# Attention and soft mixture of experts in one kernel: 2 MB transfers, half a weight tile loaded early, another order of the experts

## The chip, the cores and the metric

The kernel runs on one core of a Trainium2 chip. The metric is the device time of one execution in microseconds. Three runs of the kernel before took 131.04, 131.25 and 131.40 us; their median is 131.25 us.

## The reference

Eight batches, eight heads, 512 tokens and 32 state rows of 64 numbers each, all float32. Each token attends to the 32 state rows of its batch and head, and each state row attends to the 512 tokens. The results are laid side by side into 4608 rows of 512 numbers, (512 + 32) rows for each batch. A soft mixture of experts follows: 8 experts, 4 slots each, hidden size 1024.

```python
scores = scale * x @ state.T;  a = softmax(scores);   xread = a @ state
scores2 = scale * state @ x.T; a2 = softmax(scores2); sread = a2 @ x
z = concat([xread, sread])              # 4608 x 512
logits = z @ phi                        # 4608 x 32
slot_input = softmax(logits, axis=0).T @ z          # 32 x 512
for e in range(8):                      # 4 slots of each expert
    slot_out[e] = relu(slot_input[e] @ w1[e]) @ w2[e]
out = softmax(logits, axis=1) @ slot_out            # 4608 x 512
```

x is 8 MB, the weights w1 and w2 are 16 MB each, the output is 8.5 MB.

## The kernel before

**Stages.** Attention runs over batches 0 to 7 with its steps interleaved by hand: ORDER (lines 29 to 57) lists them as name.batch.half, and the loop at line 661 issues them in that order. `X.b.g` transposes a quarter of batch b on TensorE, `S.b` makes both kinds of scores, `R.b.h` multiplies the state rows' weights with x and is the last reader of batch b's x. The logits never leave the chip; the softmax over all rows is kept as a running maximum and sum. Every engine has its own queue and works through it in this order.

Then come the experts. `w1_part(hf, e)` multiplies one expert's slots with half of its w1 (a tile of 1 MB): 2 halves x 8 experts. Two results are kept in PSUM (`h_ps`), turned and rectified (`h_turn`, `h_relu`) into `h_m`, while VectorE, ScalarE and GpSimd make the softmax over slots (`c_max`, `c_exp`, `c_div`, `c_back`). `w2_part(k, hf, e)` then adds expert e's share to the slot outputs of column block k (four blocks of 128 columns; blocks 0 and 1 lie in the w2 tiles of half c = 0, blocks 2 and 3 in those of c = 1), using half hf of the hidden numbers. A block has 16 parts. `so_copy(k)`, `so_sum(k)` (sum over four row groups, and a copy by ScalarE) make it ready, and `out(k, q)` multiplies it with the softmax weights of half of the tokens: four matmuls into four PSUM tiles, two copies by ScalarE, two by VectorE, and the store of 1 MB. `out_st(c)` does the same for the state rows, 0.25 MB. Lines 825 to 867 hold the order of parts and outputs; `more(k, n)` issues the next n parts of block k.

**Transfers.** All loads but one and all stores are issued by SP's queue, in program order. A big buffer is 8 KB on each of 128 partitions, 1 MB; there are 21 (`NBIG`). At first two hold batch 0 (the second of them also the transposed states), seven hold batches 1 to 7 and twelve the first weight tiles. `load_w(1)` after each `R.b.1` loads the next weight tile into the buffer that is given up there (lines 347 and 348); one more follows after the last use of the states (`last`, line 660). One w2 tile goes in four pieces into small buffers of attention (`load_half`), one in two pieces into others (`load_an`). The rest are loaded as `w1_part` gives up its tiles (line 689). The weights come in the order of their use: w1 half 0, w1 half 1, w2 half 0, w2 half 1, experts 0 to 7 in each.

**Homes in PSUM.** Eight banks: `ps_s` 2, `ps_t` 3, `ps_m` 3. The four tiles of an output take two from `ps_m` and two from `ps_t`.

Of the kernel before, what the change touches and what calls it, by code (L numbers as in the profile page):

```python
# [15 lines left out]
P = 128  # L16
# [8 lines left out]
NBIG = 21  # L25
# [34 lines left out]

GROUPS = ((0, 1), (2, 3), (4, 5), (6, 7))
# [3 lines left out]
def attention_soft_moe(ctx: ExitStack, tc: tile.TileContext, x0, x, stT, phi, w1, w2, out_x, out_s):  # L65
# [11 lines left out]
    big = ctx.enter_context(tc.tile_pool(name="big", bufs=NBIG))  # L77

# [13 lines left out]
    for g, t in enumerate((xs_a, xs_a[:, head:], xs_a[:, head + first :], xs_b)):  # L92
        xg[0, g] = t[:, 0:first].rearrange("p (j c) -> p j c", j=NJ)
    for b in range(1, B):
        t = big.tile([P, 4, NJ, 2 * D], F32, tag="big", name=f"x{b}")
        xv = x[b - 1].rearrange("p (g j c) -> p g j c", g=4, j=NJ)
        for k in range(2):
            if b == 1:
                nc.sync.dma_start(t[:, 2 * k : 2 * k + 2], xv[:, 2 * k : 2 * k + 2])
        if b > 1:  # L100
            nc.sync.dma_start(t, xv)
        for g in range(4):
            xg[b, g] = t[:, g]
        if b == 1:
            nc.sync.dma_start(stT_sb[:, 1:4], stT)
            nc.sync.dma_start(phi_sb, phi)

    w1t, w2t = {}, {}
    todo = [(1, hf, e) for hf in range(2) for e in range(E)]
    todo += [(2, c, e) for c in range(2) for e in range(E)]  # L110

    def load_w2(t, c, e, ft):
        n = t.shape[1] // 256
        t = t.rearrange("p (k f) -> p k f", k=n)
        nc.sync.dma_start(t, w2[c, e, :, ft : ft + n, :])
        for i in range(n):
            w2t[c, e, ft + i] = t[:, i]

    def load_w(n):
        for _ in range(min(n, len(todo))):  # L120
            layer, i, e = todo.pop(0)
            t = big.tile([P, 2 * F], F32, tag="big", name=f"w{layer}_{i}_{e}")
            if layer == 1:
                t = t.rearrange("p (k f) -> p k f", k=4)
                nc.sync.dma_start(t, w1[i, e])
                for k in range(4):
                    w1t[i, e, k] = t[:, k]
            else:
                load_w2(t, i, e, 0)
# [36 lines left out]
    with ExitStack() as actx:  # L166
# [51 lines left out]
        def load_half():  # L218
            _, c, e = todo.pop(0)
            for ft in range(0, 8, 2):  # L220
                load_w2(half(f"w2_{c}_{e}_{ft}"), c, e, ft)

        def load_an():
            _, c, e = todo.pop(0)
            for ft in range(0, 8, 4):
                load_w2(wk.tile([P, F], F32, tag="an", name=f"w2_{c}_{e}_{ft}", bufs=AN), c, e, ft)
# [107 lines left out]
        def R_(b, h):  # L334
            r = R[b]
            if h == 0:
                r["srp"] = mtile([P, 2, D], f"sr_ps{b}")
            for j in range(NJ):
                for g in range(4):
                    pe.matmul(  # L340
                        r["srp"][32 * g : 32 * g + 32, h, :],
                        r[f"eT{h}"][:, j, 32 * g : 32 * g + 32],
                        xg[b, g][:, j, D * h : D * h + D],
                        start=(j == 0),
                        stop=(j == NJ - 1),
                    )
            if h == 1:
                load_w(1)
# [308 lines left out]
        load_w(NBIG - B - 1)  # L657
# [19 lines left out]
        def w1_part(hf, e):  # L677
            for kt in range(4):
                pe.matmul(  # L679
                    h_ps[hf][32 * kt : 32 * kt + 32, :],  # L680
                    si_m[kt // 2][:, 256 * (kt % 2) + 32 * e : 256 * (kt % 2) + 32 * e + 32],
                    w1t[hf, e, kt],
                    start=(e == 0),
                    stop=(e == E - 1),
                )
            if hf == 0 and e == 3:
                h_zero()
            else:
                load_w(1)
# [47 lines left out]
        so, so_sb, so_r = {}, {}, {}  # L737
        PART = {k: (k // 2, P * (k % 2), P) for k in range(4)}

        def w2_part(k, hf, e):  # L740
# [3 lines left out]
            for i in range(4):  # L744
# [3 lines left out]
                    w2t[c, e, 4 * hf + i][:, col : col + n],  # L748
# [4 lines left out]
        def so_copy(k):  # L753
# [4 lines left out]
            dve.tensor_copy(so_sb[c][:, col : col + n], so[k])  # L758
# [7 lines left out]
        HALVED = ((0, 0), (3, 1))  # L766

        def out(k, q):
            hf, col = k // 2, 128 * (k % 2)
            o = [(ps_t if j % 2 else ps_m).tile([P, 512], F32, tag="tr" if j % 2 else "ms", name=f"o{k}_{q}_{j}")  # L770
                 for j in range(NJ)]
# [9 lines left out]
            ot = big.tile([P, NJ, 512], F32, tag="big", name=f"out{k}_{q}")  # L781
# [115 lines left out]
```

## Time and profile before

| | |
|---|---|
| median of three runs | 131.25 us (131.04 to 131.40) |
| the profiled execution | 131.05 us |
| its span | 129.3 us |
| TensorE, matmuls | 116.3 us busy (90%) |
| VectorE | 88.1 us (68%) |
| ScalarE | 76.8 us (59%) |
| GpSimd | 45.2 us (35%) |
| DMA | 51.76 MB in 8806 packets, mean 400 GB/s |
| HBM | 42.53 MB read, 8.91 MB written |
| granted TensorE clock, mean | 0.978 |

The span is what the profiler saw between the first and the last instruction; the execution's own time is a little longer. Times below count from the start of the span. A transfer has three moments: its issue on a queue, the moving of its bytes by 16 DMA engines, and its landing, when the semaphore tells that all has arrived. The profile gives the first and the last.

### The profile page before, as it was taken

How to read it: one execution, taken by the hardware profiler on the slowest of the kernel's cores; microseconds unless marked ns; L12 is line 12 of the kernel's file. 1: busy time of each engine (PE TensorE's matmuls, PEld its weight loads, DVE VectorE, ACT ScalarE, POOL GpSimd, SP SyncE). 2: the span in 40 equal slices, each digit the busy share in tenths (PEclk: the TensorE clock that was granted, in tenths of full speed). 3: DMA queues.
4: the chain of work that ended last, by engine and by line, in shares of the span. 5: the costliest groups of instructions: out<-in, count | busy, mean ns of one | idle time of the engine just before them, and what ended most of it. 6: DMA issues, size and time to landing. Idle time of an engine off the chain costs nothing.

```text
span 129.3 us, 4981 instructions
## 1 busy us (share of the span) xinstructions
PE 116.3 (90%) x2112; PEld 82.1 (64%) x2112; DVE 88.1 (68%) x224; ACT 76.8 (59%) x187; POOL 45.2 (35%) x64
## 2 busy tenths in 40 slices
PE   6888999999999999999889899999999989898800
PEld 3527676869596976858676768963497546575300
DVE  3049999999999999999997349208950536263800
ACT  3118999999999999988985930410100425162700
POOL 2205393294575339057967113901600000000000
PEclk9999999999999999999999999999999999999965
DMA  4999999999999999999999999999999999989695
GB/s 104 382 415 426 428 423 426 421 421 426 413 431 423 421 428 421 434 416 428 418 426 423 423 403 404 402 434 423 426 421 428 423 409 397 416 325 423 287 404 214
DMA packets 8806, 51.76 MB, mean 400 GB/s; under 512 B 976, under 2 KB 1104, under 8 KB 3408
## 3 DMA queue, kind: packets, MB, share of 16 engines
q1 hardware_dynamic: 8640, 50.93, 95.3%
q10 hardware_dynamic: 144, 0.52, 1.1%
q8 instruction: 16, 0.26, 0.7%
q14 instruction: 6, 0.05, 0.1%
HBM read 42.53 MB, written 8.91 MB: 398 GB/s over the span
## 4 chain that ended last, share of the span: by engine, by line
PE 52%; DVE 32%; ACT 4%; DMA 3%; issue 3%; DVEq 0%; ACTq 0%
PE h_ps L679 11%; PE so_ps L745 11%; PE o L774 7%; PE xt_ps L232 5%; DVE q L260 5%; DVE aT L290 4%; DVE l1s L276 4%; DVE m L265 4%; DVE nm L296 4%; DMA x_a<-x_in 3%; PE sc L247 3%; PE eT_ps L315 2%; PE sr_ps L340 2%; DVE r L281 2%; PE t_ps L489 2%
## 5 line engine op out<-in xcount | busy, mean ns | idle before, releaser
L269 POOL TENSOR_TENSOR q<-q,m 128x512 f32<-128x512 f32 x16 | 16.7, 1049 | 16.1 <-DVE m L265 7.6
L238 ACT ACTIVATE xt<-xt_ps 128x512 f32<-128x512 f32 x30 | 17.9, 619 | 6.8 <-PE xt_ps L232 6.7
L285 POOL TENSOR_TENSOR q<-q,r 128x512 f32<-128x512 f32 x16 | 16.7, 1048 | 8.3 <-DVE r L281 2.7
L784 DVE COPY out<-o 128x512 f32<-128x512 f32 x16 | 10.3, 686 | 11.6 <-PE o L774 11.6
L745 PEld LDWEIGHTS so_ps<-w,h_m 128*32 128x32 f32 x512 | 13.6, 110 | 5.6 <-issue 5.3
L745 PE MATMUL so_ps<-w,h_m 128*32 128x128 f32 x512 | 16.2, 274 | 0.0
L232 PE MATMUL xt_ps<-ident,x 128*128 128x128 f32 x112 | 16.0, 277 | 0.0
L679 PE MATMUL h_ps<-w,si_m 128*32 128x512 f32 x128 | 14.4, 594 | 0.4 <-DVE si_m L643 0.4
L783 ACT COPY out<-o 128x512 f32<-128x512 f32 x16 | 8.6, 590 | 9.0 <-PE o L774 9.0
L232 PEld LDWEIGHTS xt_ps<-ident,x 128*128 128x128 f32 x112 | 12.4, 141 | 2.3 <-issue 0.8
L260 DVE STREAM_TRANSPOSE q<-sc 128x512 f32<-128x512 f32 x16 | 11.1, 694 | 1.1 <-PE sc L247 1.1
L679 PEld LDWEIGHTS h_ps<-w,si_m 128*32 128x32 f32 x128 | 9.1, 110 | 4.2 <-issue 2.6
L301 ACT ACTIVATE e<-sc,nm 128x512 f32<-128x512 f32 x16 | 11.3, 707 | 0.7 <-DVE q L260 0.4
L290 DVE STREAM_TRANSPOSE aT<-q 128x512 f32<-128x512 f32 x16 | 10.7, 687 | 0.2 <-PE sr_ps L340 0.2
L774 PE MATMUL o<-lt_all,so_r 32*128 32x512 f32 x64 | 9.9, 636 | 0.7 <-ACT so_r L764 0.7
L272 ACT ACTIVATE q<-q 128x512 f32<-128x512 f32 x16 | 10.5, 659 | 0.0
L276 DVE TENSOR_REDUCE l1s<-q 128x16 f32<-128x512 f32 x16 | 10.5, 655 | 0.1
L296 DVE TENSOR_REDUCE nm<-sc 128x1 f32<-128x512 f32 x16 | 10.5, 660 | 0.0
L265 DVE TENSOR_REDUCE m<-q 128x16 f32<-128x512 f32 x16 | 10.5, 658 | 0.0
L315 PE MATMUL eT_ps<-ident,e 128*128 128x128 f32 x64 | 9.9, 279 | 0.5 <-ACT e L301 0.5
L315 PE MATMUL an_ps<-ident,aT 128*128 128x128 f32 x64 | 9.9, 280 | 0.2 <-DVE aT L290 0.2
L332 ACT COPY an<-an_ps 128x512 f32<-128x512 f32 x16 | 9.7, 607 | 0.1
(134 smaller groups left out, 193.3 us busy)
## 6 DMA issues: line engine op xcount, KB each, us to landing
w<-w_in SPq DMA_DIRECT2D x30, 1024.0 KB, 19.4
x<-x_in SPq DMA_DIRECT2D x6, 1024.0 KB, 13.8
out_x<-out SPq DMA_DIRECT2D x6, 1024.0 KB, 5.1
out_x<-out SPq DMA_DIRECT2D x4, 512.0 KB, 5.5
x<-x_in SPq DMA_DIRECT2D x2, 512.0 KB, 6.3
w<-w_in SPq DMA_DIRECT2D x4, 256.0 KB, 12.1
w<-w_in SPq DMA_DIRECT2D x2, 512.0 KB, 7.6
x_a<-x_in ACTq DMA_DIRECT2D x1, 512.0 KB, 4.6
```

What stands on the lines that cost most here:

```text
L232: pe.transpose(p[:, P * j : P * j + P], xg[b, g][:, j, :], ident)
L238: scaled(r[f"xt{g}"], r[f"xp{g}"], 0.125)
L260: dve.transpose(r[f"q{h}"], r[f"sp{h}"])
L265: dve.tensor_reduce(out=r[f"m1{h}"], in_=r[f"qv{h}"], axis=AX.X, op=ALU.max)
L269: pool.tensor_tensor(v, v, R[b][f"m1{h}"].broadcast_to([P, 16, NS]), op=ALU.subtract)
L276: dve.tensor_reduce(out=l1s[:, i, :, 0:1], in_=R[b][f"qv{h}"], axis=AX.X, op=ALU.add)
L285: pool.tensor_tensor(v, v, R[b][f"r1{h}"].broadcast_to([P, 16, NS]), op=ALU.mult)
L290: dve.transpose(r[f"aT{h}"], r[f"q{h}"])
L315: pe.transpose(p[:, j, :], r[f"{src}{h}"][:, P * j : P * j + P], ident)
L679: pe.matmul(h_ps[hf][32 * kt : 32 * kt + 32, :], si_m[kt // 2][:, 256 * (kt % 2) + 32 * e : 256 * (kt % 2) + 32 * e + 32], w1t[hf, e, kt], ...
L745: pe.matmul(so[k][32 * i : 32 * i + 32, :], h_m[hf][:, 256 * i + 32 * e : 256 * i + 32 * e + 32], w2t[c, e, 4 * hf + i][:, col : col + n], ...
L774: pe.matmul(o[j], so_r[hf][rows, col : col + 128], lt_all[rows, 4 * q : 4 * q + 4, :].rearrange("p b s -> p (b s)"), start=True, stop=True,)
```

## The change

The 21 buffers of 1 MB become 5 of 1 MB (`big`) and 8 of 2 MB (`wide`), the same memory. Batches 3 and 4 are loaded by one transfer into one wide buffer, batches 5 and 6 into another. The host packs all weights into one array in the order of `LOADS`, so that each load reads one contiguous block. In that order the pairs come first: eleven w1 tiles (half 0, experts 5 to 7; half 1, all) and five w2 tiles (half 0, experts 0 to 4) form eight pairs, six of which are loaded at the start. Then comes `extra`, the second half (0.5 MB) of the very last w2 tile, in memory that was not used before. The w1 tiles of half 0, experts 0 to 4, follow one by one as batches 0, 1, 2, 7 and the states give up their buffers; the last two pairs follow batches 4 and 6. Later w2 tiles come single (five), in small pieces (two as before) or in pairs (two), and the first half of the very last tile is the last load.

After the experts' first layer: the parts of block 2 begin before the first output and are spread between the outputs; `so_copy(2)` moves from VectorE to ScalarE; the two q of an output block share one wide buffer; the last output's third and fourth PSUM tile come from `ps_s`; outputs (3,0) and (3,1) are stored in halves, (0,0) no longer is. `h_zero` (zeros for `h_m`) comes one expert earlier.

```diff
-NBIG = 21
+NBIG = 5
+NWIDE = 8
+PAIRS = ((3, 4), (5, 6))
+FREED = {0: "big", 1: "big", 2: "big", 4: "wide", 6: "wide", 7: "big"}
+REUSED = {(0, 0): "big", (0, 1): "big", (0, 3): "big", (0, 4): "big", (0, 6): "wide", (1, 0): "wide", (1, 2): "wide"}
+def tile_of(layer, i, e, k0=0, k=8):
+    return (layer, i, e, k0, k)
+def loads():
+    first = [tile_of(1, hf, e) for hf in range(2) for e in range(E)]
+    second = [[tile_of(2, c, e) for e in range(E)] for c in range(2)]
+    early, paired = first[:5], first[5:] + second[0][:5]
+    pairs = [("wide", paired[i : i + 2]) for i in range(0, 16, 2)]
+    yield from pairs[:6]
+    yield "extra", [tile_of(2, 1, 7, 4, 4)]
+    yield from [("big", [t]) for t in early[:3]]
+    yield from pairs[6:]
+    yield from [("big", [t]) for t in early[3:]]
+    yield "half", [second[0][5]]
+    yield "an", [second[0][6]]
+    yield from [("big", [t]) for t in (second[0][7], *second[1][:3])]
+    yield "wide", second[1][3:5]
+    yield "wide", second[1][5:7]
+    yield "wide", [tile_of(2, 1, 7, 0, 4)]
...
     for b in range(1, B):
-        t = big.tile([P, 4, NJ, 2 * D], F32, tag="big", name=f"x{b}")
...
+        if any(b == pair[1] for pair in PAIRS):
+            continue
+        pair = next((p for p in PAIRS if b in p), (b,))
+        n = len(pair)
+        t = (wide if n == 2 else big).tile([P, 2 * F * n], F32, tag="wide" if n == 2 else "big", name=f"x{b}")
+        rows = x[(b - 1) * P * 2 * F : (b - 1 + n) * P * 2 * F].rearrange("(p f) -> p f", p=P)
+        parts = 2 if b == 1 else 1
+        step = 2 * F * n // parts
+        for k in range(parts):
+            nc.sync.dma_start(t[:, k * step : (k + 1) * step], rows[:, k * step : (k + 1) * step])
...
+    def load_w(kind, tiles=None):
+        want, pieces = todo.pop(0)
+        assert want == kind
+        n = sum(k for *_, k in pieces) * F // 4
+        if kind == "wide":
+            tiles = [wide.tile([P, 4 * F], F32, tag="wide", name=f"w_{at[0]}")[:, 0:n]]
+        elif kind == "big":
+            tiles = [big.tile([P, n], F32, tag="big", name=f"w_{at[0]}")]
+        elif kind == "extra":
+            tiles = [cp.tile([P, n], F32, name="w_extra")]
+        rows = w[at[0] : at[0] + P * n].rearrange("(p f) -> p f", p=P)
+        at[0] += P * n
+        done = 0
+        for t in tiles:
+            nc.sync.dma_start(t, rows[:, done : done + t.shape[1]])
+            done += t.shape[1]
+        place(tiles, pieces)
...
-            if h == 1:
-                load_w(1)
+            if h == 1 and b in FREED:
+                load_w(FREED[b])
...
-        load_w(NBIG - B - 1)
+        for kind in ["wide"] * (NWIDE - len(PAIRS)) + ["extra"]:
+            load_w(kind)
...
             if i == last:
-                load_w(1)
+                load_w("big")
...
-            if hf == 0 and e == 3:
+            if hf == 0 and e == 2:
                 h_zero()
-            else:
-                load_w(1)
+            elif (hf, e) in REUSED:
+                load_w(REUSED[hf, e])
...
-            dve.tensor_copy(so_sb[c][:, col : col + n], so[k])
+            (act.copy if k == 2 else dve.tensor_copy)(so_sb[c][:, col : col + n], so[k])
...
-        HALVED = ((0, 0), (3, 1))
+        HALVED = ((3, 0), (3, 1))
...
-            o = [(ps_t if j % 2 else ps_m).tile([P, 512], F32, tag="tr" if j % 2 else "ms", name=f"o{k}_{q}_{j}")
-                 for j in range(NJ)]
+            homes = [(ps_m, "ms"), (ps_t, "tr")] * 2
+            if (k, q) == (3, 1):
+                homes[2:] = [(ps_s, "sc")] * 2
+            o = [pool.tile([P, 512], F32, tag=t, name=f"o{k}_{q}_{j}") for j, (pool, t) in enumerate(homes)]
...
-            ot = big.tile([P, NJ, 512], F32, tag="big", name=f"out{k}_{q}")
+            if q == 0:
+                out_t[k] = wide.tile([P, 2, NJ, 512], F32, tag="wide", name=f"out{k}")
+            ot = out_t[k][:, q]
...
         so_copy(0)
-        more(1, 4)
+        more(1, 6)
         so_sum(0)
         more(1, 2)
+        more(2, 3)
         out(0, 0)
+        more(2, 1)
         more(1, 4)
+        more(2, 1)
+        so_copy(1)
+        more(2, 1)
         out(0, 1)
-        more(1, 2)
-        so_copy(1)
+        more(2, 2)
+        so_sum(1)
         more(2, 3)
-        so_sum(1)
-        more(2, 2)
         out(1, 0)
         more(2, 5)
+        so_copy(2)
         out(1, 1)
-        more(2, 6)
-        so_copy(2)
-        more(3, 3)
+        more(3, 1)
         so_sum(2)
+        more(3, 4)
         out(2, 0)
         more(3, 5)
         out(2, 1)
-        more(3, 8)
+        more(3, 6)
         so_copy(3)
```

## Rows read from the trace of the kernel before

**Rows 1.** The page's slices: 40 equal parts of the span, rate of transfers.
```profile
GB/s 104 382 415 426 428 423 426 421 421 426 413 431 423 421 428 421 434 416 428 418 426 423 423 403 404 402 434 423 426 421 428 423 409 397 416 325 423 287 404 214
```

**Rows 2.** Stretches, attention: length, busy us of PE, PEld, DVE, ACT, POOL, PEclk, DMA share, GB/s.
```profile
26.00:65.00 39.00, 37.78 (x816) 28.78 (x814) 38.40 (x103) 37.56 (x98) 23.44 (x28) 1.00 1.01 423
```

**Rows 3.** One weight transfer each, first and sixteenth: duration ns, issue us; us to landing.
```profile
L125 SPq DMA_DIRECT2D w<-w_in x1: 328/328/328, 9.8 to 9.8; - x1
DMA to landing us min/median/max: 18.8/18.8/18.8
...
L125 SPq DMA_DIRECT2D w<-w_in x1: 328/328/328, 45.8 to 45.8; - x1
DMA to landing us min/median/max: 19.5/19.5/19.5
```

**Rows 4.** The same: a 1 MB load, the last 256 KB piece behind it, the last load.
```profile
L115 SPq DMA_DIRECT2D w<-w_in x1: 328/328/328, 67.4 to 67.4; - x1
DMA to landing us min/median/max: 11.7/11.7/11.7
...
L115 SPq DMA_DIRECT2D w<-w_in x1: 382/382/382, 69.2 to 69.2; - x1
DMA to landing us min/median/max: 12.4/12.4/12.4
...
L115 SPq DMA_DIRECT2D w<-w_in x1: 328/328/328, 86.9 to 86.9; - x1
DMA to landing us min/median/max: 19.3/19.3/19.3
```

**Rows 5.** Stretches behind the last load, the two with least moved.
```profile
114.00:115.40 1.40, 1.40 (x27) 0.44 (x20) 0.47 (x1) 0.21 (x1) 0.00 (x0) 1.00 0.56 222
...
120.80:122.00 1.20, 1.20 (x8) 0.73 (x6) 1.18 (x3) 0.96 (x3) 0.00 (x0) 1.00 0.21 80
```

**Rows 6.** One output transfer each: outputs (2,0), (3,0) and the last state output.
```profile
L789 SPq DMA_DIRECT2D out_x<-out x1: 332/332/332, 114.5 to 114.5; - x1
DMA to landing us min/median/max: 4.8/4.8/4.8
...
L789 SPq DMA_DIRECT2D out_x<-out x1: 332/332/332, 121.3 to 121.3; - x1
DMA to landing us min/median/max: 3.8/3.8/3.8
...
L805 SPq DMA_DIRECT2D out_s<-out_s x1: 1209/1209/1209, 123.5 to 123.5; - x1
DMA to landing us min/median/max: 4.7/4.7/4.7
```

**Rows 7.** Loads of batches 3 and 4; TensorE's first transpose of batch 3.
```profile
L101 SPq DMA_DIRECT2D x<-x_in x2: 328/464/600, 5.3 to 5.7; - x2
DMA to landing us min/median/max: 9.5/11.2/12.9
...
19.44 0.27 PE L232 MATMUL xt_ps<-ident,x 128*128 128x128 f32 x1
```

**Rows 8.** The chain that ended last: start us, us, engine, tile, line, count.
```profile
77.81 9.06 PE h_ps L679 x80
...
94.43 4.28 PE so_ps L745 x152
98.71 0.42 PE sum_ps L763 x2
...
111.98 1.14 PE o L774 x8
113.12 1.23 PE so_ps L745 x40
...
117.30 0.63 PE os L796 x4
```

**Rows 9.** The page's DMA queues: packets, MB, share of 16 engines' time.
```profile
q8 instruction: 16, 0.26, 0.7%
```

More of the change, by code (lines that the diff above doesn't have):

```diff
@@ L59, with attention_soft_moe @@
 AN = 2
+FREED = {0: "big", 1: "big", 2: "big", 4: "wide", 6: "wide", 7: "big"}
[18 more added lines that the diff above has]
+    yield "wide", [tile_of(2, 1, 7, 0, 4)]
+LOADS = tuple(loads())
 GROUPS = ((0, 1), (2, 3), (4, 5), (6, 7))
 @with_exitstack
-def attention_soft_moe(ctx: ExitStack, tc: tile.TileContext, x0, x, stT, phi, w1, w2, out_x, out_s):
+def attention_soft_moe(ctx: ExitStack, tc: tile.TileContext, x0, x, stT, phi, w, out_x, out_s):
     nc = tc.nc
@@ L106, in attention_soft_moe, with place @@
             nc.sync.dma_start(phi_sb, phi)
[L108 to L127, printed above, removed]
-            else:
-                load_w2(t, i, e, 0)
+    wt = {}
+    todo = list(LOADS)
+    at = [0]
+    def load_w(kind, tiles=None):
[15 more added lines that the diff above has]
+        place(tiles, pieces)
+    def place(tiles, pieces):
+        spans = [(t, c) for t in tiles for c in range(0, t.shape[1], F // 4)]
+        for layer, i, e, k0, k in pieces:
+            step = 2 if layer == 1 else 1
+            for q in range(0, k, step):
+                t, c = spans[0]
+                del spans[0:step]
+                wt[layer, i, e, (k0 + q) // step] = t[:, c : c + step * F // 4]
     def st_t(b, g):
@@ L218, in load_half @@
         def load_half():
-            _, c, e = todo.pop(0)
-            for ft in range(0, 8, 2):
-                load_w2(half(f"w2_{c}_{e}_{ft}"), c, e, ft)
+            load_w("half", [half(f"w_half{i}") for i in range(4)])
         def load_an():
-            _, c, e = todo.pop(0)
-            for ft in range(0, 8, 4):
-                load_w2(wk.tile([P, F], F32, tag="an", name=f"w2_{c}_{e}_{ft}", bufs=AN), c, e, ft)
+            load_w("an", [wk.tile([P, F], F32, tag="an", name=f"w_an{i}", bufs=AN) for i in range(2)])
         def X(b, g):
@@ L878, with block @@
     sts = con(state.reshape(4, 2, 2, 2, 2, NS, D).transpose(4, 6, 0, 3, 2, 1, 5)).reshape(P, 8 * P)
+    w1 = moe_w1.reshape(E, 4, P, 2, 512).transpose(3, 0, 2, 1, 4).reshape(2, E, P, 8, 256)
+    w2 = moe_w2.reshape(E, 8, P, 2, 256).transpose(3, 0, 2, 1, 4)
+    def block(pieces):
+        return _np.concatenate(
+            [(w1 if layer == 1 else w2)[i, e][:, k0 : k0 + k].reshape(P, -1) for layer, i, e, k0, k in pieces], axis=1
+        )
+    second = [p[1] for p in PAIRS]
+    x_loads = [(b, 2 if any(p[0] == b for p in PAIRS) else 1) for b in range(1, B) if b not in second]
     arrays = {
         "x0_in": con(_np.concatenate([xs[0, :, 0:512], sts[:, 0:256], xs[0, :, 512:]], axis=1)),
-        "x_in": con(xs[1:]),
+        "x_in": con(_np.concatenate([con(xs[b : b + n].transpose(1, 0, 2)) for b, n in x_loads], axis=None)),
         "stT_in": con(sts[:, 256:]).reshape(P, 3, 2, 2, 2, NS),
         "phi_in": con(moe_phi.reshape(4, 2, D, NS).transpose(1, 2, 0, 3)).reshape(P, 4, NS),
-        "w1_in": con(moe_w1.reshape(E, 4, P, 2, 512).transpose(3, 0, 2, 1, 4)),
-        "w2_in": con(moe_w2.reshape(E, 8, P, 2, 256).transpose(3, 0, 2, 1, 4)),
+        "w_in": con(_np.concatenate([block(p) for _, p in LOADS], axis=None)),
     }
```

21 lines of the change are left out of this document (9 added, 12 removed).

## The prediction, made before the result was known

> **What bounds the kernel now.** I read the page's slices first. The line to look at is GB/s: from the third slice to the 35th it hardly moves, and it has two holes and a short last slice near the end [rows 1]. Next the stretches: from 26 to 65 us the DMA engines are busy 1.01 of the time, and VectorE 38.40 of 39.00 us [rows 2]. So two things run flat out side by side, and the question is which of them the end hangs on. The landings answer it. The first weight lands at 9.8 + 18.8 = 28.6 us and the sixteenth at 45.8 + 19.5 = 65.3 us: 15 MB in 36.7 us, 2.44 us each [rows 3]. Those that I looked at wait 12 to 20 us behind others between issue and landing [rows 3, 4], so the queue is never empty. The last weight lands at 86.9 + 19.3 = 106.2 us, long after TensorE released its buffer [rows 4]. Outputs use the same engines. They are eight of 1 MB and two of 0.25 MB, 8.5 units, which is 8.5 x 2.44 = 20.7 us of moving. Without a hole the last would land at 106.2 + 20.7 = 126.9 us; it lands at 123.5 + 4.7 = 128.2 us [rows 6]. So 1.3 us are lost behind the weights, and the holes show where: 222 GB/s at 114.0 to 115.4 us, 80 GB/s at 120.8 to 122.0 us [rows 5]. There TensorE and the copies had not made the next output in time. The kernel is bound by its transfers, except for those 1.3 us, which are bound by the order of the work after the weights. TensorE's attention part and its expert order matter only where they delay an output or a load.
>
> **What surrounds the span.** The profiled execution took 131.05 us with a span of 129.3, so 1.75 us lie around it. The median of the runs shown is 131.25, 0.2 above. I make the sum against the profiled one and add 0.2.
>
> **The transfers in 2 MB (12 pairs become 12 transfers; the bytes stay).** What could be saved is a cost for each transfer or row. Four transfers of 256 KB landed between 67.4 + 11.7 = 79.1 and 69.2 + 12.4 = 81.6 us, 2.5 us for their 1 MB, against 2.44 us for one of 1 MB [rows 3, 4]. Three more transfers, in rows four times shorter, cost 0.06 us; since the landings are read to 0.1 us it may be 0.2. So 12 fewer save 12 x 0.02 = 0.24 us, and 0.8 at the most. Rows of 16 KB do stand in the trace, but on another queue: 16 instruction packets of 16 KB take 0.7% of 16 engines' 129.3 us, 0.9 us each [rows 9]. An 8 KB row takes 2.44 / 8 = 0.305 us on its engine, so 16 KB at that rate is 0.61 us, and 0.61 plus one 8 KB row in between is 0.915. I read the 0.9 so, as two queues taking turns, and take 0 for the size of the rows. If a 16 KB data row were itself that slow, 12 transfers x 8 rows x 0.3 us = 29 us would be added, the far upper bound; the lower is -0.8. Nearest are the 256 KB rows, on the same queue.
>
> Of a fixed price the Trainium skill ("DMA: Bandwidth & Descriptors", section "Anatomy of one DMA") says that each transfer costs about 2.0 us plus its bytes at 436 GB/s, fitted on transfers issued by GpSimd. By it the 12 pairs would give back 12 x 2.0 = 24 us, an estimate from that page. The landings 2.44 us apart [rows 3] speak against it here: whatever is fixed is paid while others move.
>
> **What a pair delays.** Batch 3 becomes usable with batch 4. In the trace those two were issued at 5.3 and 5.7 and landed 9.5 and 12.9 us later, at 14.8 and 18.6 us (the row gives both as min and max) [rows 7]. The bytes ahead are the same, so the pair lands at 18.6. TensorE's first transpose after batch 2's is batch 3's, at 19.44 us [rows 7]: 0.85 us of cover, cost 0. With the cover gone, each us late is a us for TensorE, then for VectorE, which has no idle time up to 65 us [rows 2]. Batch 5 comes with batch 6 and is used far later: 0.
>
> **The weights' order.** Now early: the pairs and half of the last expert (0.5 MB). Late: experts 3 and 4 of the first half, which become the loads after batch 7 and after step U.1. Counting MB behind x7, they are the 20th-and-a-half and 21.5th; the 21st landed at 79.1 us and the 22nd at 81.6 [rows 4], so they land at 77.9 and 80.4. TensorE starts the experts at 77.81 and takes 9.06 / 10 = 0.91 us for each [rows 8]: it wants expert 3 at 80.5 and expert 4 at 81.4. Cover 1.0 us, cost 0, and below nothing it cannot go. SP now waits for batches 4 and 6 instead of one buffer for each batch; behind those waits stand only later loads, and the queue holds more than 10 us of bytes [rows 4]. In the second layer, experts 3 and 4 of half 1 land together at 106.2 - 2.5 x 2.5 = 100.0, experts 5 and 6 at 105.0, and the last half tile at 106.2 as before.
>
> **The order after the weights, which is the term that counts.** Nineteen parts of w2 take 4.28 us and five 1.23 us [rows 8], so a run of n parts takes 0.14 + 0.218 n. An output's matmuls take 1.14, a sum 0.42, the state output 0.63 [rows 8]. The output of which the matmuls ended at 111.98 + 1.14 = 113.12 was issued at 114.5: 1.4 us of copies and issue [rows 6, 8]. From 94.43 on the new order runs: 21 parts to 99.15, sum, 5 parts, out(0,0) to 101.95; 7 parts, out(0,1) to 104.8; 2, sum, 3, out(1,0) to 107.7; 5, out(1,1) to 110.1; 1, sum, 4, out(2,0) to 113.0; 5, out(2,1) to 115.4; 6, state output, sum and its copy to 118.2; out(3,0) to 119.3; out(3,1) to 120.5; state output 121.1. The parts that need late weights ask for experts 5 and 6 at about 106.3 (landed 105.0) and the last half tile after 107.7 (106.2), so no load is waited for. Issues are then, with 1.4 us: 103.4, 106.2, 109.1, 111.5, 114.4, 116.8, state 118.0, the halves of column block 3 at 120.2, 120.8, 121.3, 122.0, state 122.4.
>
> When must they be issued? The one at 121.3 landed 3.8 us later on a nearly empty queue [rows 6]: 2.44 of moving and 1.4 before. Without holes an issue must come 1.4 us before its predecessor has landed: by 104.8, 107.3, 109.7, 112.2, 114.6, 117.0, 119.5, 120.1, 121.3, 122.6, 123.8, 125.0. All are in time but one, late by 0.1: loss 0.1, gain 1.2. But the issue at 114.5 took 4.8 us to land, 2.3 before moving [rows 6]. With 2.3 throughout, the worst is late by 1.0 and the gain is 0.3. Lateness does not add up, since one late output pushes back all behind it. Between 0.3 and 1.2 I take 0.95, nearer to the upper end, because the last four issues come 1.1 us or more earlier than now whichever holds (121.3 becomes 120.2, 123.5 becomes 122.4) and most outputs have room of 0.2 to 1.4.
>
> The rest goes together at 0: the third column block's copy moves from VectorE to ScalarE (a sum behind it starts over 1 us later), the last output's two PSUM tiles come from another pool (it no longer waits for copies; counted above), two 1 MB outputs share a 16 KB buffer without waiting for each other, and only block 3 is issued in halves.
>
> **Sum.** 0 (larger transfers) + 0 (pairs) + 0 (weights) - 0.95 (outputs): span 129.3 to 128.35, execution 130.1, median 130.3.
>
> **Rivals.** (a) Larger transfers are also faster: 0.24 to 0.8 by the count above. Then 129.5 to 130.1. For it: nothing but the 0.06 us. Against: 2.44 and 2.5 lie too close. (b) The holes only move: the outputs still come late because the copies and TensorE set the pace, not the order. For it: the 0.2 us slacks at 114.4 and 116.8. Then the gain is 0 to 0.3: 130.95 to 131.25. This is also the case that the new order doesn't do what it says. (c) Slower: 16 KB rows hold each DMA engine twice as long, so whatever takes turns with them waits for 0.61 instead of 0.305 us, and rows that long may run below 2.44 us per MB. Place: the 24 MB in pairs, 58.6 us of the queue. It decides at 1.6%: there 0.95 us are eaten, and from 2% expert 4 also comes too late for TensorE. At 5% it costs 2.9 - 0.95 = 2.0 us: 133.2. For it: the 0.9 us packets [rows 9], if not read as turns. Against: from 2 KB to 8 KB the rate does not fall [rows 3, 4].
>
> Of turns the Trainium skill ("DMA: Bandwidth & Descriptors", section "Queues, rings and completion order") says that each DMA engine goes round its queues packet by packet; 0.9 = 0.61 + 0.305 agrees [rows 9]. By that rule an instruction packet would take 1.22 us behind a 16 KB row, 0.3 more, 12 or so times; no row shows an engine waiting for one, so it stays inside (c).
>
> **Chances and range.** Forecast (130.0 to 130.8) 0.54; (a) 0.12; (b) 0.20; (c) 0.14. For this kernel 0.3% is 0.39 us, about what a measurement can tell from no change: faster means below 130.86. The forecast and (a) give 0.66, and a sliver of (b) 0.02: 0.68 faster. The rest of (b) and the mildest of (c): 0.21 same. 0.11 slower. The range 129.2 to 131.8 holds the forecast, (a), (b) and the mild part of (c), which ends at 131.8 if the rows run 2.6% slower (1.5 us on 58.6).
>
> **What would show it.** Right: landings of a 2 MB transfer 4.9 us apart; the last weight at 106.2; no stretch after it under 380 GB/s until the last output; out(0,1) issued near 106, the last state output near 122.4. Batch 3's transposes still near 19.4 and the experts' start near 77.8. Wrong: 2 MB landings 5.0 or 4.8 apart (c or a); TensorE waiting for x or for w in the experts' stretch; or holes of over 0.5 us between outputs (b).

## The result and the profile after

The changed kernel takes 132.68 us (median of four runs, 132.26 to 133.16) against 131.31 us: a ratio of 1.0109, 95% interval 1.0071 to 1.0147. It is 1.1% slower, where 130.3 us was forecast. The profiled execution took 133.16 us with a span of 131.4.

The page's rate of transfers, in 40 slices of the span, as in [rows 1]:

```profile
GB/s 113 365 394 455 429 424 412 442 434 422 427 424 434 424 424 434 402 422 439 437 429 407 417 403 408 424 427 442 427 439 412 242 299 342 422 394 412 398 412 53
```

The two small holes at 325 and 287 are gone. In their place stands one wide hole, 242, 299, 342, just where the loads end and the outputs begin. The stretches, after first and then before (length, busy us of PE, PEld, DVE, ACT, POOL, PEclk, DMA share, GB/s):

```profile
102.00:112.00 10.00, 10.00 (x203) 5.75 (x202) 4.23 (x8) 3.87 (x9) 0.00 (x0) 1.00 0.71 295
112.00:116.00 4.00, 4.00 (x94) 2.63 (x90) 2.43 (x4) 2.15 (x5) 0.00 (x0) 1.00 1.01 418
116.00:124.00 8.00, 6.44 (x82) 3.29 (x82) 4.83 (x10) 4.04 (x9) 0.00 (x0) 1.00 0.97 401
```

```profile
102.00:112.00 10.00, 9.18 (x200) 5.76 (x200) 4.48 (x9) 3.76 (x8) 0.00 (x0) 1.00 0.99 408
112.00:116.00 4.00, 4.00 (x80) 2.29 (x84) 1.81 (x3) 1.64 (x4) 0.00 (x0) 1.00 0.84 344
116.00:124.00 8.00, 5.82 (x74) 3.35 (x66) 4.39 (x9) 3.57 (x9) 0.00 (x0) 0.97 0.88 365
```

At 102 to 112 us the share falls from 0.99 to 0.71, 2.8 us of all engines' time; behind it, to 124 us, 0.17 x 4 + 0.09 x 8 = 1.4 us come back. The forecast saw what comes back and not what it costs in front.

The chain of waits, after (start us, us, engine, tile, line, count), answers to [rows 8]:

```profile
78.72 9.06 PE h_ps L721 x80
...
95.33 4.72 PE so_ps L787 x168
100.06 0.42 PE sum_ps L805 x2
100.48 0.57 PE so_ps L787 x15
101.04 0.81 issue
101.86 0.99 PE so_ps L787 x25
102.85 1.07 PE o L818 x8
```

Two things are new. The experts start at 78.72 us instead of 77.81. And in the middle of the parts ahead of the first output TensorE stands still for 0.81 us, "issue": it waits for nothing that the profile shows. No such piece stands in the chain of before from the experts on.

The last big load, the first output and the last state output (each a row and its time to landing), for [rows 4] and [rows 6]:

```profile
L163 SPq DMA_DIRECT2D w<-w_in x1: 327/327/327, 89.4 to 89.4; - x1
DMA to landing us min/median/max: 16.3/16.3/16.3
...
L835 SPq DMA_DIRECT2D out_x<-out x1: 348/348/348, 105.3 to 105.3; - x1
DMA to landing us min/median/max: 4.2/4.2/4.2
...
L851 SPq DMA_DIRECT2D out_s<-out_s x1: 1076/1076/1076, 124.7 to 124.7; - x1
DMA to landing us min/median/max: 5.7/5.7/5.7
```

The loads end at 89.4 + 16.3 us, 105.77 before rounding, 0.4 earlier than before. The last output lands at 124.7 + 5.7 us, 130.35 before rounding, 24.6 us behind them. By the forecast's own count the 8.5 MB need 20.7 us, so 3.8 us are lost there, where 1.3 were lost before. The first output is issued at 105.3 us, when nearly all loads have landed; before, its first half left at 101.6.

On TensorE the late start does not last. The last two outputs' matmuls, after and then before:

```profile
119.82 1.22 PE o L818 x8
```

```profile
118.71 2.64 PE o L774 x14
```

Counted from the experts' start, the chains begin the outputs' matmuls 2.2, 2.7, 1.8, 1.8, 0.7, 0.6 and at last 119.82 - 78.72 = 41.10 against 118.71 - 77.81 = 40.90, 0.2 us later than before. Of the three waits for copies that TensorE had before (0.46, 0.36 and 0.36 us) the new order keeps one (0.35). So with the pause of 0.81 us TensorE idles 1.17 us in all between the experts' start and the last output, and it idled 1.18 before. The last store, too, is issued only 0.2 us later when counted so. But it takes 5.7 us to land instead of 4.7 [rows 6].

A landing is the last of 16 completions, one for each DMA engine, and the trace records each. Before, all 16 engines completed the last store within 0.17 us, at 128.06 to 128.23. After, 13 of them completed it within 0.17 us, at 128.60 to 128.77, 0.5 us later than before, though the experts started 0.9 later; the other three came at 129.22, 129.78 and 130.35. So the end hangs on three engines that lag behind the rest by up to 1.6 us.

### The profile page after: what moved, and what is told of

Read it like the earlier page. It is cut to its first block, busy times and chain, and to the rows that moved or that the text cites. A ratio compares the mean times of both kernels' runs of the same rounds, so it can differ in the third digit from the quotient of the medians.

```text
span 131.4 us, 4954 instructions
## 1 busy us (share of the span) xinstructions
PE 117.7 (90%) x2112; PEld 82.7 (63%) x2112; DVE 87.9 (67%) x223; ACT 77.0 (59%) x188; POOL 45.3 (34%) x64
## 4 chain that ended last, share of the span: by engine, by line
PE 60%; DVE 26%; ACT 4%; issue 3%; DVEq 0%; ACTq 0%
PE so_ps L787 12%; PE h_ps L721 11%; PE xt_ps L273 7%; PE o L818 6%; PE sc L288 4%; DVE l1s L317 4%; DVE aT L331 4%; PE sr_ps L381 4%; PE spin L238 3%; PE eT_ps L356 3%; DVE m L306 3%; DVE q L301 3%; DVE nm L337 2%; DVE r L322 2%; DVE out L830 2%
## 5 line engine op out<-in xcount | busy, mean ns | idle before, releaser
L787 PE MATMUL so_ps<-w,h_m 128*32 128x128 f32 x432 | 14.9, 275 | 0.8 <-issue 0.8
L787 PEld LDWEIGHTS so_ps<-w,h_m 128*32 128x32 f32 x432 | 11.3, 110 | 6.7 <-issue 6.3
L364 ACT COPY eT<-eT_ps 128x512 f32<-128x512 f32 x16 | 9.6, 612 | 0.3 <-PE eT_ps L356 0.3
```

The source lines that it names most:

```text
L787: pe.matmul(so[k][32 * i : 32 * i + 32, :], h_m[hf][:, 256 * i + 32 * e : 256 * i + 32 * e + 32], wt[2, c, e, 4 * hf + i][:, col : col + n ...
```

## The experiments

Each ratio is against the kernel before on the same chip, with its 95% interval.

### Which half of the change costs

**Everything but the order.** The loads and buffers of after, the old order and the old tail:

```diff
-        (act.copy if k == 2 else dve.tensor_copy)(so_sb[c][:, col : col + n], so[k])
+        dve.tensor_copy(so_sb[c][:, col : col + n], so[k])
-        HALVED = ((3, 0), (3, 1))
+        HALVED = ((0, 0), (3, 1))
...
```

> The changed kernel's transfers and buffers, with the order after the weights, the halved outputs, the PSUM homes and the copy engine of the kernel before. Theory A (the new order makes the first output 3.7 us late, issued at 105.3 instead of 101.6 us; the DMA engines run dry and lose 1.3 us at once and 2.5 us later): first output issued by 103, time 130.3 to 131.0, below the kernel before because the weights then land at 105.8 instead of 106.2. Theory B (the 2 MB transfers and the pairs slow the kernel, the order is harmless): 132.3 to 133.0, as the changed kernel.

Measured: 132.68 us, 1.0083 (1.0051 to 1.0116).

**The order alone.** The loads and buffers of before, the new order and tail.

> The kernel before with only the new order after the weights, its halved outputs, PSUM homes and copy engine; all loads as before. Theory A: first output issued at 103.5 to 105, time 132.0 to 133.0, slower than before by 1 us or more. Theory B: 130.5 to 131.2, as my prediction had it for the order (gain 0.3 to 1.2).

Measured: 132.71 us, 1.0106 (1.0057 to 1.0156). Each half alone costs nearly as much as the whole. So neither theory is the whole, and the two losses do not add up. The experts start at 77.77 us here, as in before, and 13 engines complete the last store by 128.12, no later than there; the other three come at 128.43, 129.07 and 129.81. The chain of this kernel shows the pause too, with the loads of before, so the pause belongs to the order:

```profile
99.53 0.57 PE so_ps L745 x14
100.09 0.91 issue
101.00 1.03 PE so_ps L745 x26
```

**The tail.** Block 2's copy on ScalarE, the last output's two tiles from `ps_s`, and halves for (0,0), (3,0), (3,1); first on the run with the old order, then on the kernel before:

```diff
-        HALVED = ((0, 0), (3, 1))
+        HALVED = ((0, 0), (3, 0), (3, 1))
-            dve.tensor_copy(so_sb[c][:, col : col + n], so[k])
+            (act.copy if k == 2 else dve.tensor_copy)(so_sb[c][:, col : col + n], so[k])
+            if (k, q) == (3, 1):
+                homes[2:] = [(ps_s, "sc")] * 2
...
```

> As e1_old_order, but keeps what the change did to the last outputs: block 2 copied by ScalarE, two PSUM tiles of the last output from the other pool, block 3 in halves, and output (0,0) in halves as before. Theory A: 0.2 to 0.8 us below e1_old_order, 129.8 to 130.6. Theory B: as e1_old_order, 132.3 to 133.

> The kernel before with the new tail alone (ScalarE copies block 2, two PSUM tiles of the last output from the other pool, block 3 in halves); loads and order untouched. If the tail is a gain of its own (0.5 us between e1 and e3): 130.7 to 131.1. If it only fits the changed loads: 131.2 to 131.6.

Measured: 132.20 us, 1.0041 (1.0009 to 1.0072), and 131.04 us, 0.9967 (0.9938 to 0.9995). The tail gains 0.3 to 0.4%. What loses is the new order in front of it: 1.0106 with it, 0.9967 without, on the same loads and nearly the same tail; with exactly the same tail, in a run further down, 1.0064.

### The first outputs

**The first output three parts earlier**, on the changed kernel:

```diff
-        more(2, 3)
         out(0, 0)
-        more(2, 1)
+        more(2, 4)
```

> The changed kernel with one move: the three parts of block 2 in front of the first output go behind it. TensorE stood still for 0.8 to 1.2 us among these parts (100.8 to 101.9 us), with no tile waited for; in its place stands an instruction packet that ended moving at 100.5. Theory A with that stall as a wait for instructions: the output's slower issue covers it, so the first output comes 1.5 us earlier (0.7 for the parts, 0.8 for the stall), near 103.8, and the time falls by 0.7 to 1.5 to 131.2 to 132.0. If the stall is bound to the parts themselves: it moves behind the output, 0.7 us earlier, 132.0 to 132.5. Theory B: no change, 132.3 to 133.0.

Measured: 133.43 us, 1.0162 (1.0109 to 1.0215), a miss. The first output left at 104.3 us, 1.0 earlier than in after, and the time did not fall (after has 1.0109, and the intervals overlap). The chain still has the pause of 0.81 us, now right ahead of the output's own matmuls:

```profile
100.16 0.57 PE so_ps L787 x15
100.72 0.81 issue
101.54 0.27 PE so_ps L787
101.81 1.07 PE o L818 x8
```

The three parts moved from one side of the pause to the other.

**The first store held back**, on the kernel before, in two tries. In the first the store was only made whole; it was issued at 102.6 us and not held, so it does not test what it was meant to. In the second it goes behind the second output's:

```diff
+            if (k, q) == (0, 0):
+                held.append(ot)
+            elif (k, q) not in HALVED:
...
+            if (k, q) == (0, 1):
+                nc.sync.dma_start(out_x[0, 0], held[0].rearrange("p i s -> p (i s)"))
```

> The kernel before; only the store of output (0,0) is issued whole and just before that of (0,1), near 104.8 us instead of 101.6 and 102.2. No engine's work moves. My prediction's rule (in time if 1.4 us before the last weight's landing at 106.2): loss 0 to 0.2, 131.3 to 131.7. Theory D (the landing is that of the slowest of 16 DMA engines; the fastest have moved their part of the weights 2.7 us earlier, run dry at 103.1, lose their lead, and the instruction packets at 104 to 114 us, about 1.2 us each on one engine, then add to the end): loss 1.0 to 2.0, 132.3 to 133.3.

> The kernel before; the store of (0,0) is whole and stands behind that of (0,1) on SP's queue, so that neither is issued before about 104.8 us (e8 had not held it: it was issued at 102.6). No engine's work moves. My prediction's rule (in time if 1.4 us before the last weight's landing, 106.2): loss 0 to 0.2, 131.3 to 131.7. Theory D (most of the 16 DMA engines have moved their weights by 103 to 104 us, run dry and lose their lead; later instruction packets, 1.2 us or more on one engine, then add to the end): loss 0.8 to 2.0, 132.2 to 133.4.

Measured: 131.74 us, 1.0012 (0.9985 to 1.0038), and 132.09 us, 1.0022 (0.9998 to 1.0045). In the second the stores went out at 104.8 and 105.1 us, almost as late as in after, and it cost 0.3 us, less than Theory D wanted. A late store alone does not make the 1.4% that the order costs: here TensorE was on time, and the outputs behind it came when they had come before. In its profile two engines end up to 0.7 us behind the others, not three.

**Halves for the first output on the new order** (`HALVED` with (0,0), loads of before):

> As e2_order_only (the kernel before with the new order), but output (0,0) is stored in halves, so that its first half is issued 0.6 us earlier (103.9 instead of 104.5) and nothing else moves. Theory D: the dry time shrinks by 0.6, 132.0 to 132.5 instead of 132.7. If the dry time does not count and TensorE's stall alone costs: no change, 132.6 to 132.9.

Measured: 132.63 us, 1.0064 (1.0038 to 1.0090); without halves 1.0106, and the intervals overlap.

The end on three late engines is common to the four profiles of the new order: after, the order alone, the first output earlier and this one. In each, 13 engines complete the last store within 0.24 us, and the last of the others is 1.5 to 1.8 us behind them.

### What in the order costs, on the best version

**Best version.** The kernel before with the tail, (2,0) in halves as well, and the sum of block 2 one part earlier:

```diff
-        HALVED = ((0, 0), (3, 0), (3, 1))
+        HALVED = ((0, 0), (2, 0), (3, 0), (3, 1))
-        more(3, 3)
+        more(3, 2)
         so_sum(2)
+        more(3, 1)
```

> As e7_before_new_tail (the fastest so far), with output (2,0) also in halves and one part of block 3 between its sum and its matmuls. Theory D: the engines run dry in front of (2,0) in e7 (issued at 114.4, most engines done at 114.0); 0.6 us earlier is worth 0.2 to 0.6: 130.5 to 130.9. If TensorE's chain sets the end: 131.0 to 131.2.

Measured: 130.56 us, 0.9898 (0.9865 to 0.9930), and on another chip, further down, 0.9924 (0.9895 to 0.9952). It beats both kernels.

**Three parts ahead of its first output, taken from behind the second; the sum of block 1 now stands behind the two that are left there:**

```diff
         more(1, 2)
+        more(2, 3)
         out(0, 0)
...
-        more(2, 3)
-        so_sum(1)
         more(2, 2)
+        so_sum(1)
```

> From the best version so far (130.56 us: before's loads and order, with the new tail and with (0,0), (2,0), (3,0), (3,1) stored in halves) one edit: three parts of column block 2 (0.65 us) go ahead of the first output instead of behind the second. Outputs (0,0) and (0,1) come 0.65 us later or more, if TensorE's pause for instructions now falls on parts instead of beside the output's matmuls; (1,0) and all behind it keep their place. Theory F (what the new order costs is its late first outputs, us for us): 131.0 to 131.7. Rival G (late first outputs are made good by the rest, what costs is the later middle, (1,0) to (2,1)): 130.4 to 130.8.

Measured: 132.16 us, 1.0064 (1.0031 to 1.0096): 1.7% above the best version's first measurement, 1.4% above its second, for an edit that moves 0.65 us of matmuls and one sum and adds nothing. The chains, first of the best version, then with the three parts ahead:

```profile
99.40 0.42 PE sum_ps L763 x2
99.82 0.57 PE so_ps L745 x16
100.39 1.07 PE o L776 x8
101.46 1.20 PE so_ps L745 x32
```

```profile
98.40 0.42 PE sum_ps L763 x2
98.81 1.00 PE so_ps L745 x30
99.82 0.90 issue
100.72 0.62 PE so_ps L745 x10
101.35 1.07 PE o L776 x8
...
104.58 1.27 DVE out L786 x2
105.85 0.21 DVE so_sb L758
106.05 0.14 issue
106.19 0.47 PE sum_ps L763 x2
106.66 0.02 issue
106.69 0.27 ACT so_r L764
106.96 0.04 issue
107.00 1.14 PE o L776 x8
```

The pause is there at once, 0.90 us. A second cost is the sum of block 1, ahead of which TensorE now idles 0.68 us instead of 0.46 for VectorE's copy and which is followed by its own copy, 0.27 us, with no parts between it and output (1,0). From the sum of block 0 to the last output's matmuls the chain takes 119.85 - 98.40 = 21.45 us; in the best version 119.23 - 99.40 = 19.83. These 1.6 us are 1.2% of the time, and the rest of the 1.4 to 1.7% is no more than the two measurements of the best version differ by. The time lies above what Theory F expected, and far from G.

This is not the way in which the whole new order loses. Here TensorE stays late: it idles 2.29 us from the experts' start to the last output, 0.82 in the best version. But the 16 engines complete the last store within 0.21 us, and it lands in 4.1 us, as in the best version. With the whole new order it is the other way round: TensorE catches up, and three engines lag.

What the pause is can be counted. The trace records each matmul, each weight load and each wait for a semaphore on TensorE, and the 16 packets on the instructions' queue [rows 9]. TensorE crosses record 449 and every 256th behind it; a packet starts some time later; its block is in use at the next crossing (us):

```
                 crosses 3265   packet starts   crosses 3521   stood still before
before              95.81           98.46          100.90            0.04
best version        96.50           99.27          101.63            0.09
after               96.73           99.60          101.86            1.09 (weight load)
parts ahead         95.50           98.28          100.72            1.17 (weight load)
```

This block of 256 takes 5.1 to 5.2 us from crossing to crossing in all four, whatever is in it. (A second profile of the best version stands still for 0.20 us there.) A part of w2 is 8 matmuls and 8 weight loads in 0.218 us, so 16 parts use up a block in 3.5 us; an output has as many records as one part and takes 1.14 us. Where an output lies inside the block, its slow matmuls fill the wait. Where only parts do, TensorE stands still. The new order put the first output behind the crossing. In all five profiles with the pause, after, the order alone, the first output earlier, the halves and the three parts, it falls on the same count of records, give or take one. That explains why moving it by three parts on the changed kernel did not take the pause away: the crossing came first there too.

**The first output at after's place, all behind it at the best version's:**

```diff
-        more(1, 4)
+        more(1, 6)
         so_sum(0)
         more(1, 2)
+        more(2, 3)
         out(0, 0)
         more(1, 4)
         out(0, 1)
-        more(1, 2)
         so_copy(1)
-        more(2, 3)
+        more(2, 2)
         so_sum(1)
-        more(2, 2)
```

> The same with the first output at the very place of the new order (two more parts ahead of the sum and three behind it, 1.1 us of matmuls, and the pause), while (1,0) and all behind it stay where the best version has them. Theory F: 131.5 to 132.3, most of the way to the new order's 132.6. Rival G: 130.4 to 131.0.

Measured: 132.83 us, 1.0086 (1.0054 to 1.0119). Above Theory F's range again, and against G. The whole new order with (0,0) in halves gave 1.0064, so the first output's place and the sum of block 1 cost as much time as all of it. But the three parts lost theirs on TensorE and the whole order on lagging engines, so it is not shown that the later outputs' places have no share. "Us for us" is not the size, either: the three parts cost far more than their 0.65 us, since they brought the pause and the wait at block 1's sum along, and the two more parts only 0.2%, with overlapping intervals.

**The first output whole:**

> The best version with output (0,0) stored whole instead of in halves, so that its first bytes leave with its last copy, about 0.6 us later. On the new order halves gained 0.4% with intervals that overlap. If that was real: 131.0 to 131.4. If it was chance: 130.4 to 130.8.

Measured: 130.92 us, 0.9951 (0.9922 to 0.9980), against 0.9898 and 0.9924 in halves: 0.5 or 0.3%, with intervals that overlap. The sign agrees with the run on the new order.

### The loads

**Rows of 8 KB.** Each 2 MB transfer as two runs of 8 KB per partition; on the old order, then with the new tail:

```diff
+            if len(pieces) == 2:
+                rows = w[at[0] - P * n : at[0]].rearrange("(h p f) -> p h f", h=2, p=P)
+                nc.sync.dma_start(t.rearrange("p (h f) -> p h f", h=2), rows)
...
```

> As e1_old_order (the changed kernel's loads, the old order behind the weights), with the same 2 MB transfers in the same order, but each as two runs of 8 KB in a partition instead of one of 16 KB. Theory L (long rows: TensorE waits for an instruction packet at 19 us, and that packet waits behind 16 KB data rows; 0.4 to 0.6 us of attention): that pause shrinks from 0.79 to 0.35 us, the experts start near 77.9 instead of 78.4, and the time falls from 132.7 to 131.6 to 132.2. Rival (the pause varies by itself, and the loads cost through their order): 132.4 to 133.0.

> As e5_rows8_old_order, with the new tail of e3_old_order_new_tail (ScalarE copies block 2, the last output's other PSUM tiles, block 3 in halves). Theory L: 131.0 to 131.6, 0.5 below e5 as e3 was below e1. Rival: 132.0 to 132.4, as e3.

Measured: 132.24 us, 1.0053 (1.0030 to 1.0076), where 16 KB rows gave 1.0083; and 131.72 us, 1.0012 (0.9991 to 1.0033), where they gave 1.0041. Both times 0.3%, both times with overlapping intervals. Theory L is not settled by it. The first of these runs starts the experts at 78.25 us, where 77.9 was wanted; its pause at 19 us is 0.30 us, where the same order with 16 KB rows had 0.57, but a second one of 0.45 stands at 25.8. Nor does the start go by the rows alone: the new loads with 16 KB rows have it at 77.82 in the next run.

**The new loads under the best order**, with 16 KB rows, with 8 KB rows, and each 2 MB transfer as two of 1 MB into the same buffer; and the best version on the same chip as the last two:

```diff
-                nc.sync.dma_start(t.rearrange("p (h f) -> p h f", h=2), rows)
+                for h in range(2):
+                    nc.sync.dma_start(t.rearrange("p (h f) -> p h f", h=2)[:, h], rows[:, h])
```

> The loads of the changed kernel (2 MB transfers, pairs, 0.5 MB early, weights in their new order) with the order and tail of the best version (130.56). Theory L (the loads lose 0.3 to 0.4 us in the attention, whatever follows): 130.9 to 131.3. Rival M (they lose as much as they did on the old order, 0.5 to 0.8%, part of it through the outputs): 131.3 to 131.8. Rival N (their 0.8 us earlier weights pay once the outputs come in time): 129.8 to 130.5.

> The new loads with the best order (131.65 us, 1.0007 of before), each 2 MB transfer as two runs of 8 KB per partition instead of one of 16 KB. Theory W (rows of 16 KB cost time, since whatever shares a DMA engine with them waits longer): 131.1 to 131.4, 0.2 to 0.4% back. Rival X (the row's size is nothing; what costs is the grouping of loads and their order): 131.5 to 131.8.

> The same with each 2 MB transfer as two transfers of 1 MB: buffers, packing and order of the new loads, but the transfers of the kernel before. Theory W: as with 8 KB rows, 131.1 to 131.4. Theory Y (a transfer of 2 MB itself costs, since nothing of it can be used before all has landed and 16 engines drift apart within it): 130.6 to 131.0, most of the 1.1% back. Rival X (grouping and order): 131.5 to 131.8.

> The best version (before's loads) on the same chip as the two runs above, so that the new loads are judged against it directly. 0.987 to 0.993 of before, 130.2 to 130.9, under every theory; if it is 0.995 or more, the loads cost less than the 1.1% that two chips gave.

Measured: 131.65 us, 1.0007 (0.9979 to 1.0034); 131.33 us, 0.9987 (0.9960 to 1.0014); 130.70 us, 0.9939 (0.9915 to 0.9963); 130.71 us, 0.9924 (0.9895 to 0.9952). With transfers of 1 MB the new loads cost nothing that can be measured: grouping, order, pairs and half a tile early are free, and rival X falls. The transfers of 2 MB cost 0.5 to 0.8%, Theory Y; the interval of the 1 MB run lies clear of that with 16 KB rows and touches that with 8 KB rows at its end. The rows' part of that, 0.2%, has the sign of the 0.3% above, and is within the intervals each time.

The last state output of the 8 KB run, and of the 1 MB run:

```profile
L859 SPq DMA_DIRECT2D out_s<-out_s x1: 1086/1086/1086, 123.3 to 123.3; - x1
DMA to landing us min/median/max: 4.8/4.8/4.8
```

```profile
L861 SPq DMA_DIRECT2D out_s<-out_s x1: 1092/1092/1092, 123.8 to 123.8; - x1
DMA to landing us min/median/max: 4.1/4.1/4.1
```

With 2 MB the last output is issued 0.5 us earlier, of which 0.4 is an earlier start of the experts, and lands 0.2 us later. Its 16 completions lie 0.85 us apart at the end of the 2 MB run and 0.16 at the end of the 1 MB run: in the 2 MB run 15 engines end within 0.21 us and one 0.6 us behind them. All six runs with 2 MB and the old or the best order end with 0.85 to 0.87. What makes an engine lag was not settled: the kernel before with the new tail, all in loads of 1 MB, ended with 0.94.

## Why the prediction was wrong, point by point

**The issues came 1.9 us late; this is the step that failed first.** The sum had the first output issued at 103.4 us; it was 105.3, and the other times of that list are late by as much. The terms:

- 0.91 us at the start of the experts, 78.72 instead of 77.81. It is there within the first 8 us, before anything that the change touches. TensorE's first pieces, after and before:

```profile
1.05 4.42 PE L238 MATMUL spin<-y 128*128 128x512 f32 x6 [1.05 <-DVE y L181]
5.27 2.39 PE L273 MATMUL xt_ps<-ident,x_a 128*128 128x128 f32 x12
```

```profile
1.05 3.76 PE L193 MATMUL spin<-y 128*128 128x512 f32 x6 [1.05 <-DVE y L136]
5.24 1.50 PE L232 MATMUL xt_ps<-ident,x_a 128*128 128x128 f32 x12 [0.43 <-DMA x_a<-x_in]
```

  The same twelve transposes take 2.39 instead of 1.50 us. The trace's first record of the full granted clock (2.4 GHz) stands at 7.13 us in after and 4.01 in before; over the profiles of all runs it lies anywhere from 3.89 to 7.13 with the same instructions in front. So in this profile these 0.9 us are the luck of one execution, and the loss does not need them: the order alone, with experts from 77.77 us, was as slow. The clock is not all that moves this start, though. Two other runs with these loads have the full clock at 4.7 us and the experts at 78.4, behind a pause of 0.57 and 0.45 us at 19.2 us.
- 0.81 us of pause for instructions. The sum priced parts at 0.218 us each, from 19 parts in a row [rows 8]. Those 19 met one crossing, at 95.81 us, but its packet had started 5.5 us ahead, at 90.36. The rate holds where the next block is there already; from crossing to crossing 16 parts then take 5.1 us and not 3.5. On this the trace speaks against the Trainium skill ("Runtime: NRT & Kernel Launch", section "Instruction fetch mechanics"), which says that instructions come in blocks of 256 over a DMA queue and that the fetch is hidden by the pace of issue. The blocks agree; in the four profiles of the table the fetch is hidden only where slow instructions stand in the block.
- 0.3 us more in the five parts around the pause (0.57 + 0.99 instead of 1.23), of which the output's matmuls, 1.07 instead of 1.14, give 0.1 back.

**The lag of single engines had no term in the sum; this is the second step that failed.** The forecast took 1.4 us before the predecessor's landing as the latest good issue, and the largest lateness as the loss behind the weights, 0.1 us (1.0 with 2.3 us). Put the measured issue times into that rule, 1.4 us with 2.44 us per MB from the loads' landing on, and it gives 1.2 us for before, 0.9 for the best version and 1.4 with the three parts ahead. Lost were 1.3, 1.0 and 1.5, and in all three the 16 engines end within 0.21 us of each other. For after it gives 2.1 us, since the issues were late and the loads had landed earlier, and for the order alone 0.8; lost were 3.8 and 2.7, and there the engines end 1.75 and 1.93 us apart. In every profile of this case the loss is the rule's lateness and the spread of the last 16 completions together, to within 0.1 us. So "lateness does not add up" held, and the rule as well, as far as it went. But it took the 16 engines as one queue, and a landing is that of the slowest. The spread does not add up either: 0.85 us with the new loads alone, 1.93 with the new order alone, 1.75 with both, so the two halves' losses do not.

Why three engines lag is open. In after they do not lag from the loads. The 16 completions of the last load run from 103.0 to 105.8 us, so that 11 engines have no more to move when the first output is issued, and at its landing all 16 are within 0.53 us. The lag comes after it. Theory D wanted it from instruction packets; their count does not fit without more (last section).

So the reading that the end hangs on the transfers holds, but for the slowest of 16 engines and not for their mean. The holes did move, to the front, as rival (b) had it, but at a loss.

**Larger transfers at 0 was wrong by 0.5 to 0.8%, 0.7 to 1.0 us.** That, too, is a lag at the end, 0.85 us against 0.16, as far as the profiles show. On the queue itself rival (a) had the better price. In after the first big weight loads, 2 MB each, land from 7.9 + 23.2 = 31.1 to 10.4 + 35.1 = 45.5 us, 4.8 us apart:

```profile
L163 SPq DMA_DIRECT2D w<-w_in x4: 328/328/430, 7.9 to 10.4; - x4
DMA to landing us min/median/max: 23.2/28.7/35.1
```

Yet the gain of 0.4 us at the last weight bought nothing, since the outputs were not ready, and the transfers cost elsewhere. Rival (c) had the sign and not the mechanism: it wanted more than 2.44 us per MB, and it was 2.4. A 16 KB row took 0.61 us on its engine and an 8 KB row 0.31 (medians). Nor did instruction packets wait longer behind the long rows: they took 0.88 to 0.98 us in after and 0.88 to 0.96 before, but for one of 1.31, where (c) reckoned with 1.22.

**The covers held.** Batches 3 and 4 landed together at 5.5 + 12.1 = 17.6 us and batch 3 was wanted at 20.2. The late weights landed at 77.6 and 80.1 us, forecast 77.9 and 80.4, and were wanted at 81.4 and 82.3; the runs with 1 MB transfers show that their new order costs nothing.

**The tail was right in sign.** It gains 0.3 to 0.4%, half of the 0.95 us that was forecast for it and the order together. Spreading the tail's stores is worth having; the new order ahead of it costs 1.0 to 1.4% and undoes it twice over.

## What to carry to other kernels

Where short matmuls follow each other by the hundred, count TensorE's instructions as well as its time: here a block of 256 took 5.1 us at least, and one slow output in each block hides that. A store's lateness against the landing of what is ahead of it, at its largest, was here what late stores cost. Look beside it at the 16 completions of the last transfer, and not only at the mean rate: their spread was 0.1 to 2.0 us, and it came on top. And follow a first output's lateness from a common point to the last output: one order made it good on TensorE and another did not. A larger transfer that lands sooner is worth nothing until its reader is early, and in this kernel transfers of 2 MB cost more than those of 1 MB.

## What was not expected of the hardware

- An instruction packet of 16 KB starts 2.2 to 4.2 us behind a crossing while loads fill the engines, and 0.2 to 1.9 us behind it at 89 to 91 us and from 107 us on (the four profiles of the table). Where TensorE is waiting for it, its block is usable 2.2 to 2.5 us after its start.
- The 16 completions of one load drift apart while the queue is full, to 2.7 us at the last load of before, and draw together once the engines run dry: 0.53 us at after's first output. Then they drift again, to 2.27 at output (1,1) and 1.75 at the end, where the kernel before ends with 0.17. That the instruction packets are what holds single engines back (each occupies one engine for 0.88 us or more) is argued from their times, not tried by itself. Their count does not fit without more: behind 109 us, when after's engines are in step, two packets start, at 109.01 and 115.00 us, and three engines end late.
- The granted clock's rise varied by 3.2 us between profiled executions with the same opening. The latest, in after, comes with twelve transposes that end 0.9 us later than before.
